# Exponential table, third weight copies, scale chains, first tiles and attention casts moved in a fused kernel of infini-attention and SwiGLU

## The chip, the core and the metric

One Trainium2 chip, of which the kernel uses one core. The metric is the device time of one launch in microseconds (us). Below, PE is the matmul engine, PEld its weight loads, DVE the vector engine, ACT the engine of activations, POOL the general engine beside them, SP the engine that issues the DMAs. A PSUM bank holds 128 rows of 512 floats; there are eight, numbered 0 to 7.

## The reference

`x` has 2048 rows of D=576 columns. An attention with a running memory and a SwiGLU feed-forward read it, and a gate per row mixes them:

```
g = _sigmoid((x * gate_w).sum(-1, keepdims=True))
a = _A_ref(x, A_wq, A_wk, A_wv, A_wo, A_beta)
b = _B_ref(x, B_w_gate, B_w_up, B_w_down)     # (silu(x @ w_gate) * (x @ w_up)) @ w_down, F = 4608
return g * a + (1 - g) * b
```

`_A_ref` splits the rows into N=4 segments of L=512 and the columns into H=32 heads of 18. In each segment and head

```
logits = einsum("bhqd,bhkd->bhqk", qs, ks) * scale + mask
p = _softmax(logits);  a_dot = p @ vs
a_mem = (phi(qs) @ M) / (phi(qs) @ z + 1e-6)
o = g * a_mem + (1.0 - g) * a_dot
M = M + phi(ks)^T @ vs;  z = z + sum(phi(ks))
```

and the joined heads go through `wo`.

## The kernel before

**Start stage, 0 to 245 us.** For each segment s = 0 to 3 nine `qk` chains make queries and keys, then eight `v_step`s (n = 0 to 7) the values, each followed by a `mem_step` that multiplies the running memory. A `v_step` accumulates in one of the banks 5, 6, 7 in turn; DVE empties it at L487. Beside this, squares of the inputs and weights are collected in columns of one small tile `sc`, from which scales for the f16 operands are worked out: `power` and `reach` for the input, `weigh(i)`, `reckon(i)` and `back(i)` for block i of four feed-forward units. Each of `power`, `reach` and `weigh` begins with `across`, a matmul with a tile of ones that sums such columns over the partitions (L158); in the start stage it takes bank 7 (`lone_tile`). In `weigh` a DVE part (copy, reduce, `grade` with its two integer operations at L150 and L151) is followed by eight or seven operations on POOL (L179 to L191).

**Feed-forward, 245 to 1658 us.** It runs in two halves: half 0 for segments 2 and 3, half 1 for segments 0 and 1. Each half has 36 units f, each of 128 columns of the hidden layer. A unit forms seven products (`seven(t, j)`: six matmuls at L1391 and one at L1394, all 128x512 in f16) from sums of blocks in the manner of Strassen. The products go to bank 0 (`a`), 1 (`xx`) and 2 (`y`), and are combined by ACT and DVE between them: the first product is copied from `a` to `xx` by ACT at L1474 before a third product may be added in `a`. Behind a silu (L1491, L1493) the result is split into `hh` (ACT, L1269) and `hl` (DVE, L1272). Between the products stand eight calls of `tick`, and each runs one `beat`, which carries out work that was put off by so many beats with `defer`, then down-projection groups and steps of attention.

With q = f % 3, a unit with q = 0 (from f=3 on) is heavy: it carries sixteen down-projection groups for the three units before it (`down_groups`, L1169, banks 3 and 4; DVE adds each into `ya` at L1178, or starts it at L1176) and, in half 0, the steps of the attention (`att_gen`). A group multiplies the older two of the three units before it comes to the last one. Units with q = 1 and 2 are light in half 0. Attention steps use banks 5, 6 and 7: logits (L901, L1012), the maximum on DVE (L919, then the small steps L925 to L928 that make it into `mq`, three bf16 parts), an exponential on ACT (L1016, `pe`), a causal select on POOL (L1024), and the split of the weights into `p1` (cast on DVE, L1112, or on ACT, L1114, as `turn_of` says for each of five banks) and `p2` (POOL, L1116).

ACT holds one table of functions at a time; silu and the exponential need different ones. `exp_table` runs a dummy exponential on one column (L1384), so that the load of the table stands where it is called: before, at the end of each unit with q = 2, and behind the silu of a heavy unit.

**The down weights.** In half 0 the tile of unit f is loaded (`d_load`), its squares are summed (`d_look`, ACT, L1126), three tiles of a heavy unit's round are scaled together (`d_scale`, with an `across` of its own; `d_back`), and `d_split` makes three f16 copies `dw`: the first on ACT (L1150), the second, the rest, on DVE (L1151), the third, the first scaled by a constant, on POOL (L1152). They are stored to DRAM (`dc`) for half 1 to fetch. The weights of the products come in the same beats: sums on POOL (L369), a first part on ACT (L373), the rest on DVE (L377). Each engine works through its instructions in the order in which this code issues them, one queue for each engine.

**End, from 1658 us.** The product with `wo` and the mix with the gate.

## Time and profile before

| what | value |
|---|---|
| time, median of 3 runs | 1758.87 us (1756.79 to 1760.74) |
| the profiled execution | 1758.92 us, of which its span is 1757.2 us |
| mean granted clock of PE | 0.995 |
| busy PE, DVE, ACT, POOL | 1689.3, 1331.4, 1079.2, 946.8 us |
| DMA | 311.30 MB, mean 177 GB/s |

The span runs from the first to the last instruction. The share of busy time is a mean over stages of different kinds, so the prediction reads the stages apart. In a timeline a row gives the start, the length, the engine, the line, the operation, out<-in with partitions x elements, and, in brackets, how long the engine had been idle and whose end it waited for. Matmuls run in a pipeline, so a group's length reaches a little beyond the start of the next.

### The profile page before, as it was taken

How to read it: one execution, taken by the hardware profiler on the slowest of the kernel's cores; microseconds unless marked ns; L12 is line 12 of the kernel's file. 1: busy time of each engine (PE TensorE's matmuls, PEld its weight loads, DVE VectorE, ACT ScalarE, POOL GpSimd, SP SyncE). 2: the span in 40 equal slices, each digit the busy share in tenths (PEclk: the TensorE clock that was granted, in tenths of full speed). 3: DMA queues.
4: the chain of work that ended last, by engine and by line, in shares of the span. 5: the costliest groups of instructions: out<-in, count | busy, mean ns of one | idle time of the engine just before them, and what ended most of it. 6: DMA issues, size and time to landing. Idle time of an engine off the chain costs nothing.

```text
span 1757.2 us, 35261 instructions
## 1 busy us (share of the span) xinstructions
PE 1689.3 (96%) x12267; PEld 1096.2 (62%) x12267; DVE 1331.4 (76%) x3248; ACT 1079.2 (61%) x1933; POOL 946.8 (54%) x1244
## 2 busy tenths in 40 slices
PE   9999988999999999999999999999999999999999
PEld 7888864556555655555565566556656656655599
DVE  6787676778788777887876887788778888785565
ACT  7656567567877777667675755665655565565411
POOL 3336453467676766665763565565555565554121
PEclk9999999999999999999999999999999999999999
DMA  8666675565776675445435456775876587665544
GB/s 284 219 213 209 212 246 206 191 198 163 234 222 172 194 232 175 134 142 186 150 102 180 141 139 146 191 189 116 184 181 151 136 201 176 148 138 136 160 147 140
DMA packets 341670, 311.30 MB, mean 177 GB/s; under 512 B 193396, under 2 KB 258676, under 8 KB 341492
## 3 DMA queue, kind: packets, MB, share of 16 engines
q1 hardware_dynamic: 341492, 309.05, 61.1%
q8 instruction: 96, 1.57, 0.4%
q14 instruction: 82, 0.67, 0.1%
HBM read 183.20 MB, written 99.55 MB: 161 GB/s over the span
## 4 chain that ended last, share of the span: by engine, by line
PE 63%; ACT 11%; DVE 11%; issue 5%; POOL 4%; DMA 4%; SPq 1%; DVEq 0%; ACTq 0%; POOLq 0%
PE bank L1391 25%; PE bank L1169 18%; PE bank L223 7%; PE bank L1394 4%; PE bank L901 3%; PE bank L1012 2%; ACT L1491 2%; ACT L1384 1%; PE bank L1040 1%; ACT row L1491 1%; ACT row L1493 1%; ACT pe L1016 1%; POOL ws L369 1%; DVE ya L1178 1%; PE bank L974 1%
## 5 line engine op out<-in xcount | busy, mean ns | idle before, releaser
L1169 PE MATMUL bank<-dw,hh 128*128 128x320 f16 (+1 forms) x2304 | 436.8, 286 | 19.5 <-DVE ya L1178 15.9
L1169 PE MATMUL bank<-dw,hl 128*128 128x320 f16 (+1 forms) x1152 | 329.5, 286 | 0.8 <-DVE hl L1272 0.8
L1116 POOL TENSOR_TENSOR p<-pe,p 128x512 f16<-128x512 f32 x220 | 268.1, 1219 | 55.5 <-DVE p L1112 36.1
L1169 PEld LDWEIGHTS <-hh 128*128 128x128 f16 x2304 | 224.5, 98 | 107.4 <-issue 25.3
L1016 ACT ACTIVATE pe<-bank 128x512 f32<-128x512 f32 x220 | 130.1, 592 | 180.5 <-PE bank L1012 156.4
L1178 DVE SCALAR_TENSOR_TENSOR ya<-bank,sc,ya 128x320 f32<-128x320 f32 x352 | 177.7, 512 | 59.7 <-PE bank L1169 57.8
L1394 PE MATMUL bank<-xr,rh 128*128 128x512 f16 x504 | 191.4, 380 | 0.8 <-DMA rh<-rc 0.8
L1024 POOL TENSOR_SCALAR_AFFINE_SELECT pe<-pe 128x256 f32<-128x256 f32 (+1 forms) x220 | 91.4, 415 | 186.8 <-ACT pe L1016 175.3
L919 DVE CUSTOM_DVE_ANT_0 junk<-bank,cm 128x128 bf16<-128x128 f32 (+2 forms) x352 | 169.6, 482 | 19.1 <-PE bank L901 14.0
L1272 DVE SCALAR_TENSOR_TENSOR hl<-hh,row 128x512 f16<-128x512 f16 x144 | 122.7, 853 | 39.2 <-ACT hh L1269 39.0
L901 PE MATMUL bank<-kst,qst 108*128 108x512 bf16 (+3 forms) x512 | 124.7, 299 | 9.7 <-ACT pe L1016 7.2
L1169 PEld LDWEIGHTS <-hl 128*128 128x128 f16 x1152 | 112.4, 98 | 30.5 <-DVE hl L1272 1.5
L1152 POOL TENSOR_SCALAR dw<-dw 128x576 f16<-128x576 f16 x36 | 79.8, 2216 | 76.8 <-ACT dw L1150 76.7
L1489 DVE TENSOR_TENSOR row<-bank,row 128x512 f32<-128x512 f32 x72 | 49.7, 690 | 78.7 <-ACT bank L1488 78.7
L1012 PE MATMUL bank<-qst,kst 111*128 111x512 bf16 (+3 forms) x352 | 103.5, 301 | 0.0
L1484 ACT ACTIVATE row<-bank 128x512 f32<-128x512 f32 x72 | 42.9, 596 | 96.1 <-PE bank L1394 96.1
L223 PE MATMUL bank<-xo,qhi 128*128 128x512 f32 x288 | 92.6, 401 | 0.6 <-DVE xo L133 0.6
L467 POOL TENSOR_TENSOR q<-qr,q 128x512 bf16<-128x512 f32 x36 | 47.6, 1323 | 81.6 <-ACT q L466 71.6
L1269 ACT ACTIVATE hh<-row 128x512 f16<-128x512 f32 x144 | 89.0, 618 | 3.8 <-DVE row L1499 3.1
L1499 DVE SCALAR_TENSOR_TENSOR row<-bank,sc,row 128x512 f32<-128x512 f32 x72 | 53.9, 749 | 47.6 <-PE bank L1394 26.2
L1394 PEld LDWEIGHTS <-rh 128*128 128x128 f16 x504 | 49.4, 98 | 60.9 <-issue 1.8
L1488 ACT ACTIVATE bank<-bank 128x512 f32<-128x512 f32 x72 | 41.9, 582 | 69.8 <-PE bank L1394 67.9
(1091 smaller groups left out, 4329.9 us busy)
## 6 DMA issues: line engine op xcount, KB each, us to landing
xo<-in_wf_dram SPq DMA_DIRECT2D x65, 320.0 KB
raw<-in_wf_dram SPq DMA_DIRECT2D x72, 256.0 KB
dc<-dw SPq DMA_DIRECT2D x36, 432.0 KB
dw<-dc SPq DMA_DIRECT2D x36, 432.0 KB
rh<-rc SPq DMA_DIRECT2D x72, 168.0 KB
draw<-in_wd_dram SPq DMA_DIRECT2D x36, 288.0 KB
xo<-in_xT_dram SPq DMA_DIRECT2D x33, 256.0 KB
vd<-vps SPq DMA_DIRECT2D x8, 912.0 KB
```

Of the source, the lines that this page charges most:

```text
L223: nc.tensor.matmul(t, st[n], mv[n], start=(n == 0), stop=(n == 13))
L901: nc.tensor.matmul(t[:, c:c + w], qs[:KR, pr, P * i:P * i + P], ks[:KR, pr, 0:w], start=True, stop=True)
L919: nc.vector.tensor_tensor_reduce(junk.bitcast(BF)[:, :w], t[:, c:c + w], cm[:, L - w:L], 1.0, -3.0e38, OP.add, OP.max, m[:, k:k + 1])
L1012: nc.tensor.matmul(t[:, c:c + w], ks[:KR + 3, pr, P * j:P * j + P], qs[:KR + 3, pr, P * j:L], start=True, stop=True)
L1016: nc.scalar.activation(pe, t, AF.Exp, scale=SCALE)
L1024: nc.gpsimd.affine_select(d, d, pattern=pat, compare_op=OP.is_ge, fill=0.0, base=0, channel_multiplier=-1)
L1116: nc.gpsimd.tensor_sub(p2, pe, p1)
L1169: nc.tensor.matmul(t, p, d[:, q, cs], start=(f == CH * c and n == 0), stop=(f == CH * c + CH - 1 and n == 2))
L1178: nc.vector.scalar_tensor_tensor(ya[:, i, cs], t, inv[c], ya[:, i, cs], op0=OP.mult, op1=OP.add)
L1272: nc.vector.scalar_tensor_tensor(lo, hi, -STEP, src, op0=OP.mult, op1=OP.add)
L1391: nc.tensor.matmul(t, w[:, p, z], x[z][:, q], start=first and n == 0, stop=False, skip_group_check=True)
L1394: nc.tensor.matmul(t, rem[:, RPOS[j]], XR[j], start=False, stop=True, skip_group_check=True)
```

## The change

It has six parts.

1. `exp_table` is called behind the first bank copy of a heavy unit in half 0 instead of at the end of the unit before it. The number of table loads stays the same.
2. The third copy of the down weights goes from POOL to ACT for two tiles of three (24 of 36), and to DVE for the third (12). The ACT ones run later than the POOL ones did, in the following q = 2 unit; the store moves with the copy.
3. `weigh` is cut in two: `weigh` keeps the sum over partitions, the DVE part and one POOL operation, and the new `bound` has the rest of the POOL chain. The clamp at 2^26 and a copy fall out of the chain, which now carries its value in `ha[i]`. In half 0 the four steps stand at beats 1, 2, 6, 9 instead of 1, 5, 8 for the old three; in the start stage they move from segment 1 to segment 2, but for `weigh(0)`, which moves from n=5 to n=6 of segment 1. `reach` moves from n=4 of segment 1 to n=0 of segment 2.
4. The first three tiles of down weights are squared, scaled and split in unit 2, beats 0 to 7, instead of units 1 and 2.
5. `turn_of`: in half 0 up to unit 23 no `p1` is cast on ACT any more (two banks of five were), and in units 24 to 35 two of five are (all were). The others are cast on DVE.
6. In `d_scale` the factor TOP is folded into a later operation (one POOL operation fewer), and one operation of the end takes a factor along.

```diff
     def weigh(i, t):
-        c = 20 + 9 * i
         n = 9 if i < 2 else 8
-        e, z = sc[:, 0:n], column(9)
-        g = nc.gpsimd
-        across(t[:, :n], sc[:, c:c + n])
-        nc.vector.tensor_copy(e, t[:, :n])
+        e = sc[:, 20 + 9 * i:20 + 9 * i + n]
+        across(t[:, :n], e)
         nc.vector.tensor_reduce(sw[i], t[:, :n], axis=AX.X, op=OP.add)
         grade(sw[i], sw[i])
-        g.tensor_scalar_mul(sw[i], sw[i], TOP)
+        nc.vector.tensor_scalar_max(e, t[:, :n], 2.0 ** -40)
+        nc.gpsimd.tensor_scalar_mul(sw[i], sw[i], TOP)
+
+    def bound(i):
+        n = 9 if i < 2 else 8
+        e, z, g = sc[:, 20 + 9 * i:20 + 9 * i + n], ha[i], nc.gpsimd
         g.tensor_scalar(e, e, sw[i], sw[i], op0=OP.mult, op1=OP.mult)
...
-        g.tensor_scalar_max(z, z, 2.0 ** 26)
         g.tensor_mul(iw[i], sw[i], sx)
...
-                    if n == 7:
-                        mid.append(lambda: reckon(1))
-                    if n == 8:
-                        mid.append(lambda: back(1))
...
-                    if n == 4:
-                        reach(lone_tile([P, 4 * NT]))
-                    if n == 5:
+                    if n == 6:
                         weigh(0, lone_tile([P, 9]))
-                    if n == 6:
-                        reckon(0)
-                    if n == 7:
-                        back(0)
+                if s == 2:
+                    for k, fn in ((0, lambda: reach(lone_tile([P, 4 * NT]))), (1, lambda: bound(0)), (3, lambda: reckon(0)), (4, lambda: bound(1)),
+                                  (5, lambda: back(0)), (6, lambda: reckon(1)), (7, lambda: back(1))):
+                        if k == n:
+                            fn()
...
-            defer(3, lambda: nc.gpsimd.tensor_scalar_mul(d[:, 2], d[:, 0], 1.0 / STEP))
-            defer(4, lambda: nc.sync.dma_start(dc[f], d.rearrange("p a n -> p (a n)")))
+            if f % CH == CH - 1:
+                o, third = 3, lambda: nc.vector.tensor_scalar_mul(d[:, 2], d[:, 0], 1.0 / STEP)
+            else:
+                o, third = 3 if f < CH else 4 if f % CH else 8, lambda: nc.scalar.activation(d[:, 2], d[:, 0], AF.Copy, scale=1.0 / STEP)
+            defer(o, third)
+            defer(o + 1, lambda: nc.sync.dma_start(dc[f], d.rearrange("p a n -> p (a n)")))
...
-                plan += [(1, lambda i=i: weigh(i, ts_tile([P, 8]))), (5, lambda i=i: reckon(i)), (8, lambda i=i: back(i))]
+                plan += [(o, lambda fn=fn, i=i: fn(i)) for o, fn in ((1, lambda i: weigh(i, ts_tile([P, 8]))), (2, bound), (6, reckon), (9, back))]
...
-                    if (f == 1 and 3 <= k < 3 + CH) or (f > 1 and q == 0 and 2 <= k < 2 + CH):
-                        d_look(k - 3 if f == 1 else f + k - 2)
-                    if (f, k) == (1, 6) or (f > 1 and (q, k) == (0, 5)):
+                    if (f == 2 and k < CH) or (f > 2 and q == 0 and 2 <= k < 2 + CH):
+                        d_look(k if f == 2 else f + k - 2)
+                    if (f, k) == (2, 3) or (f > 2 and (q, k) == (0, 5)):
                         d_scale(f // CH)
-                    if (f, k) == (2, 3) or (f > 2 and (q, k) == (1, 3)):
+                    if (f, k) == (2, 7) or (f > 2 and (q, k) == (1, 3)):
                         d_back(f // CH)
-                    if f == 2 and k in (1, 3, 5) or f > 2 and (q, k) in ((1, 1), (1, 7), (2, 5)):
-                        g = k // 2 if f == 2 else f - 1 if k == 1 else f
+                    if f == 2 and k > 4 or f > 2 and (q, k) in ((1, 1), (1, 7), (2, 5)):
+                        g = k - 5 if f == 2 else f - 1 if k == 1 else f
...
-            turn_of[0] = (1, 3) if pos < 24 else (0, 1, 2, 3, 4)
+            turn_of[0] = () if pos < 24 else (1, 3)
...
             nc.scalar.activation(xx, a, AF.Copy)
+            if half == 0 and q == 0 and f:
+                exp_table()
...
-            if half == 0 and q == CH - 1 and f < FT - 1:
-                exp_table()
```

The order on ACT at the boundary from unit 8 (q = 2) to unit 9 (heavy); `bank1<-bank0` is the copy of the first product of unit 9, `hh` that of unit 8. Before:

```order
L1150 ACTIVATE dw_5306<-draw_4513,sc_87 128x576
L373 ACTIVATE wo__5335<-ws_5307,sc_87 128x512
L1384 ACT_TABLE_LOAD
L1384 ACTIVATE bg_83<-idt_80 128x1
L1474 ACTIVATE bank1_5347<-bank0_5345 128x512
L1269 ACTIVATE hh_5205<-row_5211 128x512
L1477 ACTIVATE row_5348<-bank2_5346 128x512
```

and now, where lines stand two to six earlier in the code (L1472 was L1474, L1267 was L1269, L1382 was L1384, L1144 was L1150):

```order
L1144 ACTIVATE dw_4453<-draw_3786,sc_87 128x576
L373 ACTIVATE wo__4482<-ws_4454,sc_87 128x512
L1472 ACTIVATE bank1_4493<-bank0_4491 128x512
L1382 ACT_TABLE_LOAD
L1382 ACTIVATE bg_83<-idt_80 128x1
L1267 ACTIVATE hh_4351<-row_4357 128x512
L1477 ACTIVATE row_4494<-bank2_4492 128x512
```

The bank copy stands ahead of the table load; `hh` stands behind it, as before.

DVE at the start of the `v_step`s of segment 2, where `r` at L487 empties the bank of a `v_step` and `dn` and `om` belong to the memory. Before:

```order
L469 SCALAR_TENSOR_TENSOR ph31_1787<-bank2_1769,ph31_1787 128x512
L487 TENSOR_TENSOR r1_1827<-bank6_1812,vps0_132 128x288
L560 TENSOR_SCALAR dn_1834<-bank3_1835 128x16
L561 RECIPROCAL dn_1834<-dn_1834 128x16
L562 TENSOR_TENSOR dn_1834<-dn_1834,bg_83 128x16
L564 TENSOR_TENSOR om_1833<-bank3_1835,dn_1834 128x288
L487 TENSOR_TENSOR r1_1863<-bank7_1848,vps0_132 128x288
```

and now:

```order
L469 SCALAR_TENSOR_TENSOR ph31_1757<-bank2_1739,ph31_1757 128x512
L487 TENSOR_TENSOR r1_1795<-bank6_1780,vps0_132 128x288
L167 TENSOR_REDUCE sc_87<-bank7_1801 128x4
L168 TENSOR_REDUCE sc_87<-sc_87 128x1
L169 TENSOR_SCALAR sc_87<-sc_87 128x1
L170 TENSOR_TENSOR sc_87<-sc_87 128x1
L560 TENSOR_SCALAR dn_1808<-bank3_1809 128x16
L561 RECIPROCAL dn_1808<-dn_1808 128x16
L562 TENSOR_TENSOR dn_1808<-dn_1808,bg_83 128x16
L564 TENSOR_TENSOR om_1807<-bank3_1809,dn_1808 128x288
L487 TENSOR_TENSOR r1_1837<-bank7_1822,vps0_132 128x288
```

Between the first two emptied banks stand the four operations of `reach`, and the first of them reads bank 7, which the second `v_step` fills next.

DVE in unit 9, where the down groups and the attention meet; before:

```order
L985 TENSOR_REDUCE acc_4675<-bank5_4634 128x152
L919 ISA junk_88,mb0_2465<-bank7_4679,cm_85 128x512
L919 ISA mb0_2465 128x1
L1178 SCALAR_TENSOR_TENSOR ya_2803<-bank4_4690,sc_87,ya_2803 128x256
L1489 TENSOR_TENSOR row_4502<-bank0_4499,row_4502 128x512
```

and now:

```order
L980 TENSOR_REDUCE acc_4668<-bank5_4627 128x152
L914 ISA junk_88,mb0_2463<-bank7_4672,cm_85 128x512
L914 ISA mb0_2463 128x1
L1107 CAST p1_4679<-pe_4233 128x512
L1176 SCALAR_TENSOR_TENSOR ya_2801<-bank4_4683,sc_87,ya_2801 128x256
L1489 TENSOR_TENSOR row_4494<-bank0_4491,row_4494 128x512
```

A cast that stood on ACT is now ahead of the read that frees bank 4.

More of the change, by code (lines that the diff above doesn't have):

```diff
@@ L189, in weigh @@
         g.tensor_scalar(z, z, m[3], xq, op0=OP.max, op1=OP.mult)
-        g.tensor_scalar_max(z, z, 2.0 ** 26)
         g.tensor_mul(iw[i], sw[i], sx)
     def reckon(i):
-        z, g = column(9), nc.gpsimd
-        halve(z)
-        g.tensor_scalar(hk[i], z, 4.0 * STEP * TOP, iw[i], op0=OP.mult, op1=OP.mult)
-        g.tensor_scalar(ha[i], hk[i], iw[i], 1.0 / STEP, op0=OP.mult, op1=OP.mult)
+        halve(ha[i])
+        nc.gpsimd.tensor_scalar(hk[i], ha[i], 4.0 * STEP * TOP, iw[i], op0=OP.mult, op1=OP.mult)
+        nc.gpsimd.tensor_scalar(ha[i], hk[i], iw[i], 2.0 ** 85, op0=OP.mult, op1=OP.min)
     def back(i):
@@ L1132, in d_scale @@
             grade(r, t)
-            g.tensor_scalar_mul(r, r, TOP)
             fs = range(CH * c, CH * c + CH)
@@ L1138, in d_scale @@
                 z = r[:, z[0]:z[-1] + 1]
-                g.tensor_scalar(z, z, ha[i], 2.0 ** 100, op0=OP.mult, op1=OP.min)
+                g.tensor_scalar(z, z, ha[i], TOP, op0=OP.mult, op1=OP.mult)
             g.tensor_scalar(inv[c], r[:, 0:1], r[:, 1:2], r[:, 2:3], op0=OP.min, op1=OP.min)
@@ L1554, in gated_mix @@
                     if hf == 0:
-                        nc.vector.tensor_scalar_mul(ff, ff, g1[:, tt:tt + 1])
+                        nc.vector.tensor_scalar(ff, ff, g1[:, tt:tt + 1], STEP, op0=OP.mult, op1=OP.mult)
                     nc.vector.scalar_tensor_tensor(ff[:, c], t[:, :288], gg[:, tt:tt + 1], ff[:, c],
```

## The prediction

> **What bounds the kernel now.** I read the page first, for which engine ends the span, then the busy times by stage, then what TensorE (PE) waited for in each stage, and then the timelines round those waits. The page:
>
> ```profile
> span 1757.2 us, 35261 instructions
> PE 1689.3 (96%) x12267; PEld 1096.2 (62%) x12267; DVE 1331.4 (76%) x3248; ACT 1079.2 (61%) x1933; POOL 946.8 (54%) x1244
> ```
>
> PE is busy for 1689.3 of 1757.2 us, so at most 67.9 us are gaps, and only what shortens a gap, or a stretch of low clock, can pay: the change removes no matmul. The profiled run took 1758.92 us, 1.7 us more than its span and 0.05 from the median of 1758.87, so a change of the span is a change of the median.
>
> The stages (length, then busy time of PE, weight load, DVE, ACT, POOL, then granted clock, DMA share, GB/s):
>
> ```profile
> 0.00:245.00 245.00, 231.24 (x1307) 199.67 (x1308) 175.56 (x420) 151.03 (x302) 112.14 (x140) 0.99 0.66 226
> 245.00:328.00 83.00, 74.83 (x404) 39.48 (x403) 55.41 (x116) 56.12 (x103) 29.52 (x39) 0.98 0.61 208
> 328.00:698.00 370.00, 350.74 (x2412) 205.31 (x2411) 290.57 (x704) 272.54 (x509) 250.24 (x356) 1.00 0.66 200
> 698.00:960.00 262.00, 247.01 (x1759) 148.73 (x1759) 207.56 (x432) 176.92 (x308) 157.39 (x188) 0.99 0.49 151
> 960.00:1658.00 698.00, 690.27 (x5677) 416.95 (x5675) 542.96 (x1468) 403.19 (x671) 376.69 (x496) 1.00 0.64 157
> ```
>
> The gaps are 13.8 us in the projections, 8.2 in units f=0 to 2 and the start of f=3, 19.3 up to f=23, 15.0 up to 960 us, and 7.7 in all of half 1. The change works on the first four. What PE waited for from 328 to 698, and below that from 698 to 960 (us in all, times, longest):
>
> ```profile
> PE bank L1391 <- ACT bank L1474: 9.6, 6, 1.6
> PE bank L901 <- ACT pe L1016: 4.9, 6, 0.9
> PE bank L1169 <- DVE ya L1178: 2.3, 4, 1.0
> ...
> PE bank L1169 <- DVE ya L1178: 10.7, 9, 2.8
> PE bank L1391 <- ACT bank L1474: 1.6, 1, 1.6
> ```
>
> So there are seven waits of 1.6 us for the first bank copy of a heavy unit, six for the attention copy L1016, and thirteen for the accumulation into ya.
>
> **The exponential table behind the first bank copy: -13.** The boundary from f=8 to f=9, ACT and then PE:
>
> ```profile
> 396.43 0.76 ACT L1150 ACTIVATE dw<-draw,sc 128x576 f16<-128x576 f32 x1
> 397.10 0.71 ACT L373 ACTIVATE wo__4489<-ws,sc 128x512 f16<-128x512 f32 x1
> 397.83 1.28 ACT L1384 ACT_TABLE_LOAD   x1
> 399.12 0.20 ACT L1384 ACTIVATE bg<-idt 128x1 f32<-128x1 f32 x1
> 399.23 0.58 ACT L1474 ACTIVATE bank<-bank 128x512 f32<-128x512 f32 x1
> 399.75 0.61 ACT L1269 ACTIVATE hh<-row 128x512 f16<-128x512 f32 x1
> ...
> 394.78 1.46 PE L1391 MATMUL bank<-xo,wo__4434 128*128 128x512 f16 x6
> 396.58 1.46 PE L1391 MATMUL bank<-xo,wo__4449 128*128 128x512 f16 x6
> 399.86 1.46 PE L1391 MATMUL bank<-xo,wo__4449 128*128 128x512 f16 x6 [1.61 <-ACT bank L1474]
> ```
>
> The product that started at 394.78 was in its bank by 396.3; the copy out of that bank came only at 399.23, behind L373 and 1.40 us of table load and dummy exponential (397.83 to 399.23). Without them ahead it starts at 397.83 and ends at 398.41, where PE ends its second product at about 398.1: of 1.61 us some 0.3 stay. PE lost more than that wait: its first two products stand 1.80 us apart where one takes 1.46 plus 0.22 or less for the residual matmul, another 0.3 us, while ACT waited on weights that came through POOL. POOL is relieved there:
>
> ```profile
> 389.66 0.23 POOL L181 TENSOR_SCALAR sc<-sc 128x1 f32<-128x1 f32 x1 [0.94 <-DVE sc L151]
> 392.59 0.19 POOL L191 TENSOR_TENSOR sc<-sc 128x1 f32<-128x1 f32 x1
> L1152 POOL TENSOR_SCALAR dw<-dw x36: 1647/2272/2298, 276.9 to 939.4; 128x576 f16<-128x576 f16 x36
> ```
>
> The scale chain (389.66 to 392.78) becomes a beat later and one instruction shorter, and the weight copy of 2.27 us leaves POOL altogether, so I take 1.85 of the 1.6 + 0.6 us per boundary, seven times: 13.0. Bounds: 7 x 2.2 = 15.4, and 7 x 0.6 = 4 if the next copies on ACT are late instead. Those are hh (399.75 before) and its partner on DVE. hh still stands behind the same table load and comes at about 399.9 in either order, while PE gets to the down groups that read it 1.6 us earlier; they start with the two older tiles (some 1.6 us of matmuls), so hh ends just in time. That margin is about 0.2 us.
>
> **Third weight copies off POOL: inside the terms above.** 24 of the 36 copies go to ACT. No row shows such a copy there: L1150, same size with f32 in, takes 0.76; L1474, 512 columns, 0.58; I take 0.65. Two fall into each q=2 unit, 1.3 us, at beats where ACT waits for PE or for weights. 12 go to DVE: between the two rows below for 512 columns from f32 it is a cast of 0.42 us, or like the scalar_tensor_tensor of the same tile at 0.82; as one input less is read I take 0.42, 5 us in all and in no wait. The store to DRAM on SP's queue moves by one beat; only half 1 reads it. What DVE's extra work costs PE at unit ends, 0 to 3, I put at +1.
>
> **Attention casts from ACT to DVE: -2.5 and -7.5.** Of 65 casts on ACT 48 move: 22 in f=6 to 21, mostly four a unit, 24 in f=24 to 33, six a unit, and two at the start of half 1:
>
> ```profile
> L1112 DVE CAST p<-pe x155: 383/421/1362, 364.6 to 1620.6; 128x512 f16<-128x512 f32 x155
> L1151 DVE SCALAR_TENSOR_TENSOR dw<-draw,sc,dw x36: 809/820/1220, 277.4 to 939.3; 128x576 f16<-128x576 f32 x36
> ...
> 415.60 0.62 ACT L1114 ACTIVATE p<-pe 128x512 f16<-128x512 f32 x1
> 421.58 0.27 PE L901 MATMUL bank<-kst,qst 108*128 108x256 bf16 x1 [0.91 <-ACT pe L1016]
> ```
>
> In f=9 a cast of 0.62 stands on ACT ahead of two table loads and of the copy for which PE waits at 421.58; ACT runs without a break there, so the wait falls by up to 0.62. Five times 0.5: -2.5 (0 to -4.9).
>
> In f=24 to 33 the casts on ACT let POOL's subtraction run beside the small DVE steps that make a query's maximum. The same cast in the stage 328 to 698 and then 698 to 960 (DVE busy, mean ns), and the wait that follows:
>
> ```profile
> L927 DVE CAST mq<-mr 128x8 bf16<-128x8 f32 x10 | 1.9, 188 | 0.3
> L927 DVE CAST mq<-mr 128x8 bf16<-128x8 f32 x8 | 7.1, 884 | 0.3
> ...
> 787.82 0.69 PE L1169 MATMUL bank<-dw,hh 128*128 128x320 f16 x2 [2.80 <-DVE ya L1178]
> 787.00:794.00 7.00, 6.18 (x20) 2.91 (x20) 3.55 (x9) 1.72 (x3) 1.56 (x2) 0.51 0.12 37
> ```
>
> 188 ns became 884: DVE is held while POOL works, ya is late, and PE waits 2.80 us, after which 7 us run at a clock of 0.51: 6.18 us of matmuls that would be 3.1. With the casts on DVE, POOL starts its subtraction only when DVE gets to them. I take half of the 10.7 us of waits (5.4) and 0.7 of the 3.0 us of half clock (2.1): -7.5; bounds 0 and -13.
>
> On that clock the Trainium skill, page "TensorE: Matmul & The Clock Gate", Part 1, says that the clock halves after an idle window of about 3.4 us. Here it followed a wait of 2.80, so the trace differs; by the rule the slow stretch need not go with the wait, and the sum would be 2 us higher.
>
> **First tiles a unit later: -2.5.** In f=1:
>
> ```profile
> 267.95 0.44 PE L158 MATMUL bank<-sc 128*128 128x3 f32 x2 [4.00 <-ACT junk L1126]
> 268.25 2.72 PE L1391 MATMUL bank<-xo,wo__2939 128*128 128x512 f16 x6
> ```
>
> The column sum waits 4.00 us for three squares that stand behind a silu table load on ACT, and the six matmuls after it take 2.72 instead of 1.46, with the residual one 1.5 in all. In f=2 the squares come before the silu, so the sum waits some 0.3. But the three tiles are split at beats 5 to 7 of f=2 instead of 1 to 5, and the groups at the start of f=3 read them: late next is the third copy of the last tile, which I put at 2.5 (nearest: the 2.80 above). -4.0 - 1.5 + 0.3 + 2.5 = -2.7, taken as -2.5 (0 to -5.5).
>
> **The start stage: +2 and +0.5.** The scale chain there takes bank 7 at other chains:
>
> ```profile
> 102.52 0.38 PE L158 MATMUL bank<-sc 128*128 128x1 f32 x2 [1.71 <-DVE r L487]
> ...
> 165.04 0.45 DVE L487 TENSOR_TENSOR r<-bank,vps 128x288 f32<-128x288 f32 x1
> 165.54 3.09 PE L223 MATMUL bank<-vw,xo 128*128 128x288 f32 x12 [2.66 <-DVE r L487]
> ```
>
> A column sum that wants bank 7 right behind a v chain in it waits till DVE has read that chain, 1.71 at 102.52. For s=1 the sum of weigh moves from n=5, where bank 7 was free, to n=6, where it follows such a chain: +2 (0 to +4 with a stretch at half clock). In s=2 eight POOL instructions of weigh become one, so POOL and the DVE work that waits for it come up to 2.6 us earlier and the 2.66 at 165.54 shrinks; but reach now takes bank 7 at n=0, and the next v chain there must wait for reach's reduction, which stands on DVE behind that same late L487. -3.2 + 3.7: +0.5 (-4 to +3).
>
> **The sum.** -13.0 + 1.0 - 2.5 - 7.5 - 2.5 + 2.0 + 0.5 = -22.0. 1757.2 - 22.0 = 1735.2, and with the 1.7 round the span 1736.9: **1737**.
>
> **Rivals.**
>
> DVE becomes the bound of the heavy units, and the kernel slower. The 48 casts now stand on DVE ahead of the reads that free banks 3 and 4, and one cast can take 1.36 us beside POOL. If each of the 48 costs PE the mean of half 1 (501 ns, below), 24 us go: 1761. It decides from 22 / 48 = 0.46 us of PE wait per cast. For it: thirteen such waits are there already. Against it: DVE has 7 of 27.2 us free in f=9, where ACT has 4, and in half 1, where nearly all casts stand on DVE, PE waits for ya 2.9 us in all:
>
> ```profile
> L1112 DVE CAST p<-pe 128x512 f16<-128x512 f32 x122 | 60.9, 501 | 0.0
> 394.76:421.99 27.23, 24.58 (x196) 16.00 (x195) 20.22 (x52) 23.14 (x45) 16.12 (x26) 1.00 0.71 213
> PE bank L1169 <- DVE ya L1178: 2.9, 6, 0.9
> ```
>
> The Trainium skill, "GPSIMD Engine Reference", Specifications, says that POOL shares its SBUF interfaces with VectorE, with contention when DVE runs in a two-port mode or reads two SBUF inputs. The 1362 ns beside a median of 421 agree; by that rule more casts on DVE mean more such meetings, which raises this rival from what the half-1 row alone gives. I give it 0.10.
>
> The boundary wait only moves: hh or hl come late by what the copy gains. The margin of 0.2 is against me; that ACT has spare time once POOL is relieved is for me. The term falls from 13 to 4: 1746. Chance 0.12.
>
> The change doesn't do what it seems to in f=24 to 33: ya's reads are late anyway because the casts take DVE as much time (6 x 0.42 = 2.5 us a unit) as the stretched steps did (two chains, 2 x 0.7 for L927 alone). The 7.5 are gone: 1744 to 1745. Chance 0.13.
>
> In the start stage both moved sums wait and halve the clock, +7 instead of +2.5: 1742. Chance 0.05.
>
> **How the numbers follow.** The forecast has 0.60; its own range is 1730 to 1742. The range, down to the case in which the boundaries give 15, f=24 to 33 give 11 and the first tiles 5 (1726), and up past the two middle rivals with a unit or two of DVE waits (1752), leaves out most of the first rival. A measurement of this kernel tells 0.2%, 3.5 us, from no change. Slower: 0.08 from the first rival and 0.01 from unlucky sums; same: 0.02 from it and 0.03 from several rivals together; faster 0.86.
>
> **What would show it.** Right: no wait for the first bank copy at the seven boundaries, with the table load behind it and hh at the old distance from the next group; the mq cast near 0.2 us in f=24 to 33, with waits for ya halved and no 0.5 clock in f=27; no 4 us wait in f=1, and a wait at the start of f=3 in its place; a new wait of 1.7 us at the column sum of weigh in s=1. Wrong: many waits for ya spread over f=3 to 21 (the first rival), waits of the first groups for hh or hl of about 1.3 us at each boundary (the second), or a start stage that ends over 5 us later.

## The result and the profile after

The changed kernel takes 1744.08 us (median of 4 runs, 1741.06 to 1746.6), the kernel before 1759.21 us in the same comparison; the ratio is 0.9915, with an interval of 0.9892 to 0.9937. It is faster by 15 us: inside the whole predicted range of 1726 to 1752, outside the forecast's own range of 1730 to 1742, and short of the 22 us of the sum. The profiled execution, the slowest of the four, has a span of 1744.9, 12.3 us less than the 1757.2 before, and all stage figures below are of that execution. Its page begins:

```profile
span 1744.9 us, 35235 instructions
PE 1687.0 (97%) x12267; PEld 1096.0 (63%) x12267; DVE 1358.8 (78%) x3308; ACT 1068.8 (61%) x1909; POOL 877.2 (50%) x1187
```

POOL has lost 69.6 us of work, DVE has gained 27.4, ACT has lost 10.4. To see where the time came from, both kernels are cut at the same places: the first bank copies (L1474, now L1472) of f=0, f=4, f=24 and of the first unit of half 1. Busy time by stage, before (us, then PE, PEld, DVE, ACT, POOL busy, clock, DMA share, GB/s):

```profile
0.00:245.10 245.10, 231.24 (x1307) 199.67 (x1308) 175.56 (x420) 151.13 (x303) 112.14 (x140) 0.99 0.66 226
245.10:317.00 71.90, 63.83 (x353) 34.49 (x353) 48.21 (x105) 46.66 (x89) 26.00 (x36) 0.98 0.62 211
317.00:697.60 380.60, 361.74 (x2463) 210.30 (x2462) 297.46 (x714) 281.50 (x522) 253.36 (x358) 1.00 0.66 200
697.60:959.90 262.30, 246.91 (x1759) 148.63 (x1759) 207.85 (x435) 177.22 (x309) 157.79 (x189) 0.99 0.49 151
```

and the changed kernel:

```profile
0.00:248.80 248.80, 231.69 (x1307) 200.47 (x1308) 176.80 (x420) 151.70 (x303) 112.39 (x138) 0.98 0.66 223
248.80:317.80 69.00, 62.43 (x352) 34.05 (x352) 47.71 (x106) 47.80 (x90) 19.29 (x31) 1.00 0.64 220
317.80:687.80 370.00, 361.79 (x2463) 209.81 (x2462) 317.18 (x742) 277.36 (x513) 213.41 (x325) 1.00 0.67 205
687.80:948.20 260.40, 245.88 (x1759) 148.15 (x1758) 216.23 (x464) 170.39 (x293) 136.07 (x172) 0.99 0.49 152
```

The start stage is 3.7 us longer, f=0 to 3 are 2.9 shorter, f=4 to 23 are 10.6 shorter, f=24 to 35 are 1.9 shorter, half 1 and the end 0.6. In the last of these rows two things cancel: f=24 to 34 take 227.5 instead of 232.3, and f=35 takes 33.0 instead of 30.0. PE's busy time hardly moves; the gaps do. What PE waited for, from 328 to 690 and from 690 to 950 us of the changed kernel:

```profile
PE bank L1389 <- ACT bank L1472: 3.6, 7, 0.7
PE bank L896 <- ACT pe L1011: 2.3, 6, 0.4
PE bank L1167 <- DVE ya L1176: 1.6, 2, 0.8
PE bank L896 <- DMA kst<-stk: 0.8, 2, 0.6
...
PE bank L1167 <- DVE ya L1176: 9.1, 11, 1.6
PE bank L1167 <- DVE hl L1270: 1.8, 1, 1.8
```

The boundary waits are down from 11.2 to 3.6 us, the attention copy's in the first stretch from 4.9 to 2.3, but the waits for ya after f=24 only from 10.7 to 9.1, and one for hl is new. Why the boundary keeps 0.47 us stands in the timeline of f=8 to f=9, ACT, then DVE, then PE:

```profile
396.28 0.71 ACT L373 ACTIVATE wo__4482<-ws,sc 128x512 f16<-128x512 f32 x1
398.01 0.58 ACT L1472 ACTIVATE bank<-bank 128x512 f32<-128x512 f32 x1 [1.02 <-DVE row L1499]
...
396.41 0.84 DVE L1145 SCALAR_TENSOR_TENSOR dw<-draw,sc,dw 128x576 f16<-128x576 f32 x1 [0.70 <-ACT dw L1144]
397.17 0.74 DVE L1499 SCALAR_TENSOR_TENSOR row<-bank,sc,row 128x512 f32<-128x512 f32 x1
...
398.64 1.46 PE L1389 MATMUL bank<-xo,wo__4442 128*128 128x512 f16 x6 [0.47 <-ACT bank L1472]
```

ACT is now ready 1.02 us before the copy starts. The copy goes from bank 0 into bank 1, and bank 1 still holds the last product of the unit before, until DVE has read it at L1499; L1499 stands behind the second weight copy L1145, which in turn waits for ACT. In f=24 to 34 the small mq step is as short as it was hoped, while the casts there now stand on DVE (groups of 690 to 950 us; busy, mean ns, idle before):

```profile
L1107 DVE CAST p<-pe 128x512 f16<-128x512 f32 x24 | 11.6, 483 | 0.0
L922 DVE CAST mq<-mr 128x8 bf16<-128x8 f32 x8 | 1.4, 171 | 0.3
```

171 ns instead of 884. The start stage has the largest single wait of the changed kernel (PE, then DVE):

```profile
163.31 3.25 PE L223 MATMUL bank<-vw,xo 128*128 128x288 f32 x12 [5.92 <-DVE sc L167]
...
155.83 2.88 DVE L137 SCALAR_TENSOR_TENSOR xr<-xr,sc,xr 128x512 f16<-128x512 f32 x1
162.73 0.45 DVE L487 TENSOR_TENSOR r<-bank,vps 128x288 f32<-128x288 f32 x1
163.09 0.17 DVE L167 TENSOR_REDUCE sc<-bank 128x4 f32<-128x20 f32 x1
```

`reach` has its sums in bank 7; DVE comes to their reduction (L167) only behind a queue in which one operation alone took 2.88 us, and the second v chain wants bank 7. Then the twelve matmuls run at low clock (0.50 from 161.9 to 168.7 us): 3.25 us, where such a chain took 1.75 to 1.84 in segment 0 of the kernel before. And f=35 (PE, DVE, POOL):

```profile
928.92 0.31 PE L1167 MATMUL bank<-dw,hl 128*128 128x320 f16 x1 [1.80 <-DVE hl L1270]
...
925.87 1.10 DVE L1500 SCALAR_TENSOR_TENSOR row<-row,sc 128x512 f32<-128x512 f32 x1
926.89 1.37 DVE L1147 TENSOR_SCALAR dw<-dw 128x576 f16<-128x576 f16 x1
928.18 1.28 DVE L1270 SCALAR_TENSOR_TENSOR hl<-hh,row 128x512 f16<-128x512 f16 x2
...
924.93 3.16 POOL L1350 TENSOR_TENSOR raw<-raw 128x512 f32<-128x512 f32 x2 [15.30 <-DMA raw<-in_xr_dram]
```

The third weight copy stands on DVE ahead of hl, and DVE is stretched there while POOL adds: over all units the median of L1500 is 0.74 us, that of L1147 0.30.

### The profile page after: what moved, and what is told of

It is laid out like the page before. It is cut to its first block, busy times and chain, and to the rows that moved or that the text cites. A ratio compares the mean times of both kernels' runs of the same rounds, so it can differ in the third digit from the quotient of the medians.

```text
span 1744.9 us, 35235 instructions
## 1 busy us (share of the span) xinstructions
PE 1687.0 (97%) x12267; PEld 1096.0 (63%) x12267; DVE 1358.8 (78%) x3308; ACT 1068.8 (61%) x1909; POOL 877.2 (50%) x1187
## 3 DMA queue, kind: packets, MB, share of 16 engines
q8 instruction: 96, 1.57, 0.4%
## 4 chain that ended last, share of the span: by engine, by line
PE 64%; DVE 11%; ACT 10%; issue 5%; POOL 5%; DMA 3%; SPq 2%; DVEq 0%; ACTq 0%; POOLq 0%
PE bank L1389 25%; PE bank L1167 18%; PE bank L223 6%; PE bank L1392 4%; PE bank L896 3%; PE bank L1007 2%; POOL ws L369 1%; PE bank L1035 1%; ACT L1491 1%; DVE ya L1176 1%; ACT row L1491 1%; ACT row L1493 1%; ACT L1382 1%; DMA xo<-in_xT_dram 1%; ACT dw L1144 1%
## 5 line engine op out<-in xcount | busy, mean ns | idle before, releaser
L1111 POOL TENSOR_TENSOR p<-pe,p 128x512 f16<-128x512 f32 x220 | 272.4, 1238 | 78.4 <-DVE p L1107 46.3
L914 DVE CUSTOM_DVE_ANT_0 junk<-bank,cm 128x128 bf16<-128x128 f32 (+2 forms) x352 | 169.3, 481 | 15.1 <-PE bank L896 9.2
L1270 DVE SCALAR_TENSOR_TENSOR hl<-hh,row 128x512 f16<-128x512 f16 x144 | 128.2, 891 | 46.2 <-ACT hh L1267 45.1
L369 POOL TENSOR_TENSOR ws<-raw 128x256 f32<-128x256 f32 x72 | 65.6, 911 | 74.3 <-DMA raw<-in_wf_dram 49.5
L1107 DVE CAST p<-pe 128x512 f16<-128x512 f32 x203 | 101.8, 502 | 0.0
L1267 ACT ACTIVATE hh<-row 128x512 f16<-128x512 f32 x144 | 89.1, 619 | 4.6 <-DVE row L1499 3.1
L1499 DVE SCALAR_TENSOR_TENSOR row<-bank,sc,row 128x512 f32<-128x512 f32 x72 | 53.8, 748 | 43.2 <-ACT row L1491 21.3
```

The lines of the kernel that those rows point to most:

```text
L914: nc.vector.tensor_tensor_reduce(junk.bitcast(BF)[:, :w], t[:, c:c + w], cm[:, L - w:L], 1.0, -3.0e38, OP.add, OP.max, m[:, k:k + 1])
L1107: nc.vector.tensor_copy(p1, pe)
L1111: nc.gpsimd.tensor_sub(p2, pe, p1)
L1270: nc.vector.scalar_tensor_tensor(lo, hi, -STEP, src, op0=OP.mult, op1=OP.add)
```

## The experiments

Each is the changed kernel with the edit shown. Times are medians beside the kernel before in the same session (1758.63, 1762.03, 1757.63 and 1760.41 us in four sessions); stages are from first bank copy to first bank copy in each kernel's own profile. The start stage came out at 246.7 to 249.7 us in the eleven kernels that share it (mean 247.9), so a difference below 3 us there says nothing; in the same way f=0 to 3 took 67.9 to 70.9 us in the six kernels that share the code of those units. Part 6 of the change has no run of its own.

**The table at its old place** (`undo_table`).

```diff
-            if half == 0 and q == 0 and f:
-                exp_table()
...
+            if half == 0 and q == CH - 1 and f < FT - 1:
+                exp_table()
```

> The changed kernel with the exponential table loaded again at the end of each q=2 unit, all else as changed. Theory A (the table load ahead of the first bank copy is what PE waited for): the wait for that copy at the seven boundaries comes back from 0.47 to 1.4 us or more, and the units f=5 to f=23 lengthen by 1.2 to 1.6 us a boundary, 8 to 11 us in all: about 1753. Theory B (POOL's relief alone brought the gain; the bank copy now waits for DVE to read bank 1 at L1499, so the table load fits into that idle time of 1.02 us): under 0.5 us a boundary, 0 to 3 us in all: 1744 to 1747.

Measured: 1744.89 us (ratio to before 0.9921, 0.9904 to 0.9938), the time of the changed kernel. f=4 to 23 take 371.6 instead of 369.9, with a boundary wait of 0.88 us: the q=2 units are 0.4 us longer each, the heavy ones shorter. f=24 to 34 take 226.5 instead of 227.5. Theory B holds for the time: the part that names the change is by itself worth nothing that can be measured.

**Third copies back on POOL** (`undo_third`).

```diff
-            if f % CH == CH - 1:
-                o, third = 3, lambda: nc.vector.tensor_scalar_mul(d[:, 2], d[:, 0], 1.0 / STEP)
-            else:
-                o, third = 3 if f < CH else 4 if f % CH else 8, lambda: nc.scalar.activation(d[:, 2], d[:, 0], AF.Copy, scale=1.0 / STEP)
+            o, third = 3, lambda: nc.gpsimd.tensor_scalar_mul(d[:, 2], d[:, 0], 1.0 / STEP)
```

> The changed kernel with all 36 third copies of the down weights on POOL again at the old beat. Theory A (the copy on DVE is what makes hl late in f=35, and elsewhere the move is neutral): the 1.80 us wait for hl and the low clock in f=35 go, 3 us shorter there, nothing over 0.3 us a boundary elsewhere: about 1741. Theory B (POOL's copy delayed the weight sums at the boundaries): each boundary costs 0.5 us or more again, 4 to 8 us in all against the 3 gained: 1745 to 1749.

Measured: 1745.05 us (0.992, 0.9901 to 0.9938). f=35 takes 29.99 us with a wait for hl of 0.28, as theory A has it; f=4 to 23 take 370.7, 0.8 more, with 0.2 us a q=2 unit; f=0 to 3 take 69.6. The 3 us gained in f=35 don't show in the time; in the profile 1.3 us of them went in half 1, which has the same code, and 0.9 in the start stage, which has it too. So this run doesn't tell whether the move is worth anything elsewhere, only that it is under 1 us in f=4 to 23.

**Casts as before** (`undo_casts`).

```diff
-            turn_of[0] = () if pos < 24 else (1, 3)
+            turn_of[0] = (1, 3) if pos < 24 else (0, 1, 2, 3, 4)
```

> The changed kernel with turn_of as before: two of five p1 casts on ACT up to f=23, all five in f=24 to 35. Theory A (casts on ACT stretch the mq steps and hold up L1011): the mq cast L922 goes from 171 ns back to over 800 in f=24 to 33, the wait of L896 for the attention copy from 0.40 to 0.9 in f=9 to 21 (2.5 us in all), and f=24 to 34 lengthens by some 5 us: 1750 to 1752. Theory B (the exact time at which POOL's subtraction meets the mq steps was chance, and the gain in f=24 to 33 came from POOL's relief): the mq cast stays under 300 ns and only the 2.5 us come back: about 1746.

Measured: 1753.65 us (0.997, 0.9959 to 0.9981), theory A and somewhat more. Its groups and waits from 690 to 950 us:

```profile
L922 DVE CAST mq<-mr 128x8 bf16<-128x8 f32 x8 | 6.9, 868 | 0.3
...
PE bank L1167 <- DVE ya L1176: 13.0, 11, 2.8
```

The mq cast is back at 868 ns, the wait for ya at 13.0 us, f=24 to 34 take 231.4, and the attention copy costs up to 0.9 a heavy unit again (4.9 in all). This smallest edit is the part with the largest effect: 9.6 us between the medians, 5.5 between the spans, and 4.0 and 1.9 in the two stages that it touches (f=24 to 34 and f=4 to 23). The wait of 2.8 us in f=27 is back as well, but without the half clock that followed it before the change: f=27 takes 40.9, against 42.0 before and 38.9 changed.

**`reach` at its old place** (`undo_reach`).

```diff
+                    if n == 4:
+                        reach(lone_tile([P, 4 * NT]))
                     if n == 6:
                         weigh(0, lone_tile([P, 9]))
...
-                    for k, fn in ((0, lambda: reach(lone_tile([P, 4 * NT]))), (1, lambda: bound(0)), ...
+                    for k, fn in ((1, lambda: bound(0)), ...
```

> The changed kernel with reach back at n=4 of segment 1. Theory A (the 5.92 us wait in segment 2 is for reach's reduction in bank 7): the wait goes down to at most 1 us and the low clock behind it goes too, while segment 1 gets at most 1 us; unit f=0 starts 5 to 8 us earlier than the 248.8 of the changed kernel: 1736 to 1739. Theory B (DVE is late there in any case, through its 2.88 us operation beside POOL): PE waits 2.5 us or more for L487 at the next chain instead, and f=0 starts 2 to 3 us earlier: about 1741.

Measured: 1739.78 us (0.9892, 0.9865 to 0.9919). f=0 starts at 240.9, 8.0 us earlier than in the changed kernel's profile and 5.8 before the earliest of those that share its start. What PE waited for up to 241 us:

```profile
PE bank L223 <- DVE r L487: 2.3, 2, 1.3
PE bank L158 <- DVE gl L491: 1.8, 1, 1.8
PE bank L158 <- DVE r L487: 1.7, 1, 1.7
```

Theory A: the 5.92 us wait is gone and what comes for L487 in its place is at most 1.3. The two sums that follow a v chain in bank 7 (`power` at n=3, `weigh(0)` at n=6) still wait 1.7 and 1.8. So the rest of the move to segment 2 was good (240.9 against 245.1 before), and the place of `reach` turned it into a loss. Between the medians the gain is only 4.3 us, since the changed kernel's profile is that of its slowest run.

**First tiles as before** (`undo_first`).

```diff
-                    if (f == 2 and k < CH) or (f > 2 and q == 0 and 2 <= k < 2 + CH):
-                        d_look(k if f == 2 else f + k - 2)
+                    if (f == 1 and 3 <= k < 3 + CH) or (f > 1 and q == 0 and 2 <= k < 2 + CH):
+                        d_look(k - 3 if f == 1 else f + k - 2)
...
```

(and in the same way `d_scale`, `d_back` and `d_split`, as in the minus lines of the change)

> The changed kernel with the first three tiles of down weights squared in f=1 and split in f=2 as before, third copies where the change has them. Theory A (the move was worth the 4.0 us wait and the half clock, less what f=3 now waits for dw): the wait in f=1 is back, f=1 to f=3 is 2 to 4 us longer: 1746 to 1748. Theory B (with POOL and DVE relieved, the squares come early enough in f=1 too): no wait over 1 us in f=1, and f=3 loses its 1.7 us of waits for dw: about 1742.

Measured: 1748.97 us (0.9932, 0.9908 to 0.9955), a little beyond theory A: f=1 takes 17.4 us instead of 10.5, f=2 and f=3 together 44.5 instead of 46.7, 4.7 us in all.

**The last third copy on ACT** (`f35_scalar`).

```diff
+            if f == FT - 1:
+                o, third = 2, lambda: nc.scalar.activation(d[:, 2], d[:, 0], AF.Copy, scale=1.0 / STEP)
-            if f % CH == CH - 1:
+            elif f % CH == CH - 1:
```

> The changed kernel with the third copy of the last tile, f=35, on ACT a beat earlier, where ACT is idle for 1.55 us. Theory A (the DVE copy ahead of hl is the cause of the wait of 1.80 us for hl and of the clock of 0.95 in f=35): the wait falls to 0.3 and f=35 from 32.98 to about 30: 1741. Theory B (hl is late through hh and row, and waits in any case): f=35 shortens by under 1 us: 1743 to 1744.

Measured: 1744.82 us (0.9906, 0.9877 to 0.9935), f=35 at 32.76: theory B, and mine fell. The timeline of f=35, DVE and POOL:

```profile
924.31 1.10 DVE L1502 SCALAR_TENSOR_TENSOR row<-row,sc 128x512 f32<-128x512 f32 x1
925.33 2.35 DVE L1272 SCALAR_TENSOR_TENSOR hl<-hh,row 128x512 f16<-128x512 f16 x2
...
923.49 3.04 POOL L1352 TENSOR_TENSOR raw<-raw 128x512 f32<-128x512 f32 x2 [15.42 <-DMA raw<-in_xr_dram]
```

With no copy ahead of them the two hl still take 2.35 us, and PE waits 1.58. What makes them late is POOL: relieved of the weight copy, it starts the sums of the next half (L1352, L1350 above) beside DVE's row and hl. Before the change the POOL copy (2.28 us) kept these sums back until 941.64, and the first hl was through in time. All fourteen profiles agree: in the four where POOL's sums start behind DVE's second row (the kernel before, `undo_third`, `undo_three` and `spread_second` below) f=35 takes 29.8 to 30.0 us, in the ten where they start ahead of that row 31.3 to 34.7.

**The second copy a beat later** (`late_second`).

```diff
-            defer(2, lambda: nc.vector.scalar_tensor_tensor(d[:, 1], r, k, d[:, 0], op0=OP.mult, op1=OP.subtract))
+            defer(3 if f % CH == CH - 1 and f > CH else 2, lambda: nc.vector.scalar_tensor_tensor(d[:, 1], ...))
```

> The changed kernel with the second copy of the last tile of each three (DVE, L1145) one beat later, so that L1499 and L1500 stand ahead of it. Theory A (what is left of the boundary wait is bank 1, which L1499 reads behind L1145): the wait of 0.47 for the first bank copy and the 0.7 us at the end of q=2 units go, 1.0 us a boundary, 6 to 8 us in all: 1736 to 1738. Theory B (the weight sums on POOL, one behind the other, set the pace at the boundary): the bank copy comes earlier but PE waits for its weights, under 0.4 us a boundary: 1741 to 1744.

Measured: 1742.49 us (0.9895, 0.9864 to 0.9927). Theory A at the boundaries: no wait for the first bank copy is left, and f=4 to 23 take 363.8, 6.2 less. The time keeps only part of it, since from f=24 on the later copy is in the way: the waits for ya grow from 9.1 to 10.4 us, and in f=35 PE waits 2.21 us for the copy itself (L1145), so that f=24 to 34 take 229.0 instead of 227.5 and f=35 34.7 instead of 33.0.

**The feed-forward chain in its old beats** (`undo_chain`).

```diff
-   ... in ((1, lambda i: weigh(i, ts_tile([P, 8]))), (2, bound), (6, reckon), (9, back))]
+   ... in ((1, lambda i: (weigh(i, ts_tile([P, 8])), bound(i))), (5, reckon), (8, back))]
```

> The changed kernel with the POOL chain of the feed-forward scales (bound) again in the same beat as weigh, reckon at beat 5 and back at beat 8. Theory A (the beat of the chain matters to the weights at the boundary): q=2 units lengthen by 0.3 us or more, 2 to 4 us in all: 1746 to 1748. Theory B (with the third copy off POOL there is room for the chain anywhere): no unit changes by over 0.2 us: 1744.

Measured: 1742.06 us (0.9896, 0.9872 to 0.9921); f=4 to 23 take 369.6, q=2 units 11.41 instead of 11.51. Theory B: with the third copy off POOL the beat doesn't matter to more than 0.1 us a unit.

**Does the table's place matter once bank 1 is free early?** (`second_table`: the edit of `undo_table`, and)

```diff
-            defer(2, lambda: nc.vector.scalar_tensor_tensor(d[:, 1], ...))
+            defer(3 if f % CH == CH - 1 and CH < f < 24 else 2, lambda: nc.vector.scalar_tensor_tensor(d[:, 1], ...))
```

> The changed kernel with the second copy of the last tile a beat later in f=5 to 23, and the exponential table loaded at the end of the q=2 unit as before the change. The table's old place cost nothing while bank 1 was freed late. Theory A (the two are in series, and the earlier table pays once L1499 is early): the first bank copy is again late by part of the 1.48 us of load and dummy, PE waits 0.6 to 1.2 us for it at seven boundaries, and f=4 to 23 takes 368 to 371 instead of 363.8: 1741 to 1745. Theory B (the table's place does not matter here at all): f=4 to 23 takes 364 to 365.5: 1737 to 1738.

Measured: 1745.44 us (0.9924, 0.9897 to 0.995); f=4 to 23 take 371.9. What PE waited for from 328 to 685 us begins:

```profile
PE bank L1389 <- ACT bank L1472: 5.2, 6, 0.9
```

Theory A. With bank 1 freed early, the table's old place costs 371.9 - 363.8 = 8.1 us; with bank 1 freed late, 1.7. The copy starts at the later of two things, ACT's table and DVE's read, so to mend one alone shows next to nothing: with the old place of the table the late copy gains nothing at all (371.9 against 371.6).

**Three parts undone at once** (`undo_three`: the edits of `undo_table`, `undo_third` and `undo_chain` together).

> The changed kernel with three parts undone at once: the table at the end of the q=2 unit, all third copies on POOL, the POOL chain of the feed-forward scales at the old beats. Each alone changed f=4 to 23 by under 2 us. Theory A (they stand in for one another: either the table's place or POOL's relief brings ACT in time): the wait of 1.6 us for the first bank copy is back at seven boundaries, q=2 units take 13.0 us and f=4 to 23 takes 377 to 379, of 369.95 in the changed kernel and 380.66 before; with f=35 at 30: 1749 to 1751. Theory B (what shortened the boundaries is the casts or something else): f=4 to 23 under 373: 1743 to 1746.

Measured: 1746.98 us (0.9939, 0.9921 to 0.9958). f=4 to 23 take 373.5, the boundary wait is 1.3 us, q=2 units take 12.41. More than each alone, less than theory A: some 0.6 us a boundary against the kernel before was still unexplained. The chain on POOL took 2.50 us there, where it took 3.12 before.

**One POOL operation more** (`undo_three_max`: `undo_three`, and)

```diff
         g.tensor_scalar(z, z, m[3], xq, op0=OP.max, op1=OP.mult)
+        g.tensor_scalar_max(z, z, 2.0 ** 26)
```

> The kernel with the three parts undone, and the clamp at 2^26 put back in POOL's chain (one POOL operation more). With the three undone, a boundary is still 0.6 us shorter than before the change, and the chain on POOL there takes 2.50 us where it took 3.12. Theory A (every part of a us that POOL's chain is shorter comes off the boundary, since ACT's weight copy waits for the POOL sum behind it): q=2 units go from 12.41 to 12.7 or more, 0.3 us for the operation and its gap, 2 us over seven boundaries, and 0.3 more if the operation of 8 columns in the chain meets DVE again: 1749. Theory B (the rest comes from the casts on DVE): q=2 units stay at 12.4: 1747.

Measured: 1750.21 us (0.9937, 0.9919 to 0.9954), q=2 units at 12.80, f=4 to 23 at 376.2. What PE waited for from 328 to 690 us begins:

```profile
PE bank L1387 <- ACT bank L1470: 10.3, 6, 1.7
```

Theory A: one operation of 0.21 us with its gaps makes the chain 0.40 us longer (2.90 instead of 2.50) and costs 0.39 us at each of seven boundaries, 2.7 us in f=4 to 23. What is still missing to the 12.99 us of the kernel before, 0.19, is about what the chain is still shorter than its 3.12; no run tests that rest.

**Put together** (`spread_second`).

```diff
-                    if n == 3:
+                    if n == 4:
                         power(sx, lone_tile([P, 1]))
-                    if n == 6:
+                    if n == 5:
+                        reach(lone_tile([P, 4 * NT]))
+                    if n == 7:
                         weigh(0, lone_tile([P, 9]))
...
+            defer(3 if f % CH == CH - 1 and CH < f < 24 else 2, lambda: nc.vector.scalar_tensor_tensor(d[:, 1], ...))
+            if f == FT - 1:
+                o, third = 3, lambda: nc.gpsimd.tensor_scalar_mul(d[:, 2], d[:, 0], 1.0 / STEP)
```

> A version put together from the runs before it: the changed kernel with power, reach and weigh(0) at n=4, 5 and 7 of segment 1 (never behind a v chain in bank 7), the second copy of the last tile a beat later in f=5 to 23 only, and the third copy of f=35 on POOL. Theory A (the three causes are separate and add): f=0 starts at 240 or before (8 earlier, with the 5.9 us wait and the two of 1.5 and 1.7 gone), f=4 to 23 take 363.8 as with the second copy late, f=35 takes 30.0; in all 8 + 6 + 3 = 17 us off 1744: 1727 to 1730. Theory B (DVE is late in the start stage wherever the sums stand, and f=35 depends on when POOL's sums of the next half meet DVE): f=0 starts at 241 to 243, f=35 stays above 31: 1732 to 1735.

Measured: 1725.37 us (ratio to before 0.9814, 0.979 to 0.9838), beyond theory A: 18.7 us less than the changed kernel between the medians, 18 by the two ratios. f=0 starts at 237.5, f=4 to 23 take 363.5, f=35 takes 29.8, and PE's mean clock is 1.000. The three causes add up: 11.3 + 6.4 + 3.2 = 20.9 of the 21.6 us between the two spans.

## Why the prediction was right, and where its terms were off

**The boundaries, -13, the argument half wrong.** Measured in the waits, 11.2 became 3.6, and the two products ahead of it stand 1.51 us apart instead of 1.80, 0.3 us seven times: -9.6. The lengths of the seven q=2 units say the same, -10.2. The step that failed is "Without them ahead it starts at 397.83": it looked at ACT's queue alone. The copy's target is bank 1, and in the kernel before DVE read that bank late too (timeline of DVE before the change):

```profile
397.23 0.82 DVE L1151 SCALAR_TENSOR_TENSOR dw<-draw,sc,dw 128x576 f16<-128x576 f32 x1 [1.10 <-ACT dw L1150]
397.97 0.74 DVE L1499 SCALAR_TENSOR_TENSOR row<-bank,sc,row 128x512 f32<-128x512 f32 x1
```

With this order on DVE the copy could not have come before 398.71, wherever the table load stood. `second_table` and `late_second` show the two lower bounds in turn. The chain on POOL was counted as one of the reliefs; that the boundary pays its full length, 0.39 us for one operation, was not seen. The margin of 0.2 us for hh was too small for what follows hh: behind the table load DVE's hl is late, and the weight load of the third group waits for it in all six heavy units from f=6 to 21 (PEld's waits from 317.8 to 687.8 us, then the one in f=9):

```profile
PEld L1167 <- DVE hl L1270: 2.0, 6, 0.3
401.40 0.10 PEld L1167 LDWEIGHTS <-hl 128*128 128x128 f16 x1 [0.34 <-DVE hl L1270]
```

PE's list of waits doesn't show this; in f=9 the third group's matmuls with hl start 0.44 us behind those with hh instead of 0.27, so that PE loses 0.17. With the table at its old place (`undo_table`) this wait is gone.

**The attention copy, -2.5.** 4.9 became 2.3 us, and `undo_casts` brings it back: the wait was right. The heavy units of f=6 to 21 are nevertheless only 0.6 us shorter in all. In f=9 the copy's wait is 0.51 shorter and the unit 0.35, as 0.17 go at hl; f=6 and f=12 even became longer, by 0.9 and 0.1, with new waits for the DMAs of `kst` and `qst` late in the unit (up to 0.84).

**f=24 to 33, -7.5, the mechanism right, the size wrong.** The mq cast fell from 884 to 171 ns, and f=27, which had the half clock, went from 42.0 to 38.9 us. Of these 3.1 us, 2.0 come back with `undo_casts` and 1.1 don't: the wait of 2.8 us is there again, but no slow stretch follows it. So the part of the term that stood for the clock rested on a stretch that doesn't come with every such wait. (The row of ten mq casts in the prediction is from 365 to 700 us; from 328 to 698 there are twelve, 186 ns on average.) But the waits for ya fell by 1.6 us in place of 5.4. The rival had named a reason: 24 casts, 11.6 us of DVE time, took the place of the stretched steps; no run separates the two. f=24 to 34 gained 4.8, of which 1.3 lies in the three q=2 units and comes with the table (`undo_table` gives it back): -3.5. The casts were nonetheless the best part, as their undoing costs 4.0 us here.

**f=35, not in the sum, +3.0.** "12 go to DVE ... in no wait" was wrong for the last of them, and not because of the copy. POOL's free time was taken to be free of cost; in f=35 the sums that POOL then starts earlier stretch DVE's row and hl. That is worth 1.4 us: `undo_reach` and `undo_casts` have the same late hl and take 31.3 and 31.4 us. The other 1.6 are a stretch of 3.4 us at half clock behind the wait of 1.80 us, which those two kernels don't have.

**First tiles, -2.5.** f=0 to 3 gained 2.9, within the 0.9 to 3.9 of the six kernels with the same code there. The new waits came where they were expected, at the first groups of f=3 for dw, 1.7 us in two pieces in place of 2.5.

**Start stage, +2.5, measured +3.7 (+2.7 by the mean of the eleven profiles).** `weigh(0)` waits 1.5 in segment 1 where 2 were reckoned. For `reach` the place and the reason were right (bank 7, DVE late), the wait was 5.92 plus a low clock instead of 3.7.

The rivals: DVE didn't become the bound of the heavy units up to f=21 (1.6 us of waits for ya, 2.3 before), as the few waits of half 1 had led to expect. The boundary rival, a wait that moves, came true in part: 0.47 us of it moved to bank 1 and 0.17 to hl, which it had named. The medians differ by 15.1 us, the profiled spans by 12.3. By lengths of units the sum of -22 was 9.7 us too good on the span: 2.8 in the q=2 units of f=5 to 23, 1.9 in the heavy units of f=6 to 21, 2.7 in f=24 to 34, 3.0 in f=35 and 1.2 in the start stage; against that stand 0.3 at the first tiles, 0.6 in half 1 and the end, and the 1.0 reckoned for DVE's extra work at unit ends. So nearly every term was too good, and the range was wide enough to hold that.

## What to carry to other kernels

A copy waits for its target as well as for its source and its engine: before an instruction is moved ahead in its queue, look when the bank that it writes is freed, and by whom. When two late things end at the same moment, undoing either shows nothing, so a part with no effect by itself may be worth 8 us next to another; tests in pairs tell. A list of the matmuls' waits is not complete: a late weight load shows in PEld's. Time taken off an engine is used at once by what is queued there next, and that may meet another engine at a worse place.

## What the runs showed of the hardware that was not expected

DVE and POOL hold each other up, and which of them is held can change with nothing in the order or the start times to tell why. The last weight copy on POOL and the second one on DVE (with the row after it) in two kernels with the same order on both engines there, `undo_three`:

```profile
926.37 0.82 DVE L1145 SCALAR_TENSOR_TENSOR dw<-draw,sc,dw 128x576 f16<-128x576 f32 x1 [1.53 <-ACT dw L1144]
927.77 0.74 DVE L1495 SCALAR_TENSOR_TENSOR row<-row,sc 128x512 f32<-128x512 f32 x1
...
926.42 2.28 POOL L1146 TENSOR_SCALAR dw<-dw 128x576 f16<-128x576 f16 x1 [7.03 <-ACT dw L1144]
```

and `undo_three_max`:

```profile
927.55 1.32 DVE L1146 SCALAR_TENSOR_TENSOR dw<-draw,sc,dw 128x576 f16<-128x576 f32 x1 [1.53 <-ACT dw L1145]
929.46 1.57 DVE L1496 SCALAR_TENSOR_TENSOR row<-row,sc 128x512 f32<-128x512 f32 x1
...
927.60 1.65 POOL L1147 TENSOR_SCALAR dw<-dw 128x576 f16<-128x576 f16 x1 [7.03 <-ACT dw L1145]
```

In both POOL starts 0.05 us after DVE. In the first it takes 2.28 us while DVE runs at its usual speed; in the second POOL takes 1.65 and DVE 1.32 for the operation of 0.82, then the row meets POOL's next sum and takes 1.57. In the profiles of all fourteen kernels POOL starts 0.05 to 0.06 us behind DVE 71 times, and 70 times POOL is the one held (2.27 to 2.31 us, DVE 0.82). Where POOL starts half a us ahead, 46 times, both are longer (2.11 to 2.19 and 1.21 to 1.22). f=35 takes 30.0 us in the one kernel and 32.3 in the other, though the edit adds nothing to that unit: `undo_three_max` carries 2.3 us there that aren't the price of its operation. The Trainium skill, "GPSIMD Engine Reference", Specifications, says that POOL shares its SBUF interfaces with VectorE, with contention when a DVE instruction has two SBUF inputs or runs in a two-port mode. These rows agree, since the second copy reads both `draw` and `dw`, and they add that either engine can be the one that loses.

The clock: apart from stretches at the very end of a kernel, every slow stretch in the fourteen profiles ran at 0.50 and lasted 3.4 or 6.8 us, such as 161.9 to 168.7 in the changed kernel, round the end of the 5.92 us wait. A wait alone doesn't tell whether one comes. The 2.80 us wait in f=27 before the change was followed by 6.8 us at half clock, the 2.81 us wait there in `undo_casts` by none; the wait for hl of 1.80 us in f=35 of the changed kernel was followed by 3.4 us of it, that of 1.83 in `undo_reach` by none, nor were the seven boundary waits of 1.6 us before the change. What else decides stays open. `spread_second`, in which PE's longest wait is 1.61 us, ran at full clock until its last 0.2 us.
